# Batch 0's values through a casting DMA, key sums from a column of ones, and one copy moved to VectorE, in a fused attention and swish-MLP kernel

## The chip, the cores and the metric

The kernel runs on one core of one Trainium2 chip. The time is the device time of one execution in microseconds; the figure given for a kernel is the median of several runs. TensorE (PE) multiplies matrices, its weight loads are listed as PEld; VectorE (DVE), ScalarE (ACT) and GpSimd (POOL) work on tiles in SBUF and PSUM; SyncE (SP) issues most of the DMAs.

## What is computed

Linear attention over 8 batches, 8 heads, 576 positions and head size 64, whose result goes through an MLP with a swish that has a slope of its own for each of 2048 hidden columns:

```python
q_s = exp(q - max(q, -1)); q_s = q_s / sum(q_s, -1)      # softmax over the 64 channels
k_s = exp(k - max(k,  2)); k_s = k_s / sum(k_s,  2)      # softmax over the 576 positions
kv  = einsum('bhsd,bhse->bhde', k_s, v)
x   = einsum('bhsd,bhde->bhse', q_s, kv)                 # -> 4608 tokens x 512
h   = x @ w_in                                           # 512 -> 2048
out = (h * sigmoid(beta * h)) @ w_out                    # 2048 -> 512
```

All inputs and the output are float32 in DRAM; the kernel multiplies in bf16 and leaves the two maxima out, which cancel.

## The kernel before, in words

**Tiles.** A batch's 8 heads are handled as 4 pairs (`hp` 0 to 3). K and V of a pair lie as 128 partitions x 9 blocks (`NG`) x 64. `KF`, `VF`, `QF` hold the float32 inputs of a batch (two buffers each, chosen by the batch's parity), `EK` and `EQ` the bf16 exponentials, `VB` the bf16 values. A row of `VB` is `VW` = 66 wide: 64 values and two more that GpSimd sets to one (L230), so that one matmul with 65 columns gives K^T V and, in column 64, the sum of the keys. `kvd` (L391) scales the product by the reciprocal of that sum into `KVD`; `out_mm` (L426) multiplies it with the transposed queries `QT` into a 128 x 512 piece of `XT`, one for each pair. `pass1_mm` (L627) multiplies the four pieces of `XT` with `WIN` into the 16 tiles of h (`f` 0 to 15), ScalarE makes the swish of each (L637), `pass2_group` (L706) multiplies with `WOUT`. The nine slabs `t` are the eight batches' first 512 positions, and slab 8 the positions that are left over.

**Order.** Nothing is scheduled by the machine: each engine runs its instructions in the order in which the program adds them, and `Program` (L46) works out which semaphores an instruction waits for from the keys that it reads and writes. The attention of a later batch is woven into the matmuls of an earlier slab: `todo` holds pairs of a slot number and a step, and `tick` (L740) runs the steps that are due after each matmul.

**Batch 0, the head of the kernel.** There is no earlier slab to hide it in. SP issues Q in 4 chunks (L283), K in 4 (L529), beta (L532) and V in 4 (L534). `exp_q` and `exp_kh` run on ScalarE (L594 to L600), `norm_main` (L322) divides the queries by their sums: a reduction and a reciprocal on VectorE, a multiplication on VectorE or, for pairs 1 and 3, on GpSimd (L602, L608). `t_steps` (L364) transposes a pair on TensorE and copies it to `QT`. Key sums are taken apart from the products here: `ksum` (L500) multiplies by column 64 of `VB` alone, `ksum_inv` (L506) takes reciprocals. V is turned to bf16 by `cast_v` (L343): pairs 0 and 1 on VectorE, 2 and 3 on ScalarE (L621 to L623). `kv_mm` (L511) makes the products. `warm` (L493) issues matmuls whose result nobody reads.

**The weights.** `load_win` (L556) brings w_in in five pieces through DMAs issued on GpSimd that turn float32 into bf16; the first waits for the last chunk of batch 0's K. Piece 0 has columns 0 to 255 (`f` 0 and 1), piece 1 the next 256, pieces 2 to 4 have 512 each (`f` 4 to 7, 8 to 11, 12 to 15). `load_wout` (L539) on SP brings w_out as float32; its first DMA waits for piece 2 of w_in (`wgate`, L561), and behind it on SP are the loads of batch 1 (L764 to L768) and of the later batches. `scale_wout` (L546) multiplies w_out on VectorE by the reciprocal of beta.

**Slab 1.** `attn_late(2)` (L483) prepares batch 2 beside slab 1's second matmuls. Its four copies of PSUM to `XT` run on VectorE for pairs 0 to 2 and on ScalarE for pair 3 (L487). In front of the latter in ScalarE's order stand the exponentials of batch 3 (L801 to L809).

Of the kernel before, what the change touches and what calls it, by code (L numbers as in the profile page):

```python
# [158 lines left out]
def bass_efficient_attn_shen__then__act_swish_beta_kernel(  # L159
# [12 lines left out]
    with ExitStack() as es:  # L172
        def sb(name, shape, dt):
            return es.enter_context(nc.sbuf_tensor(name, shape, dt))
# [33 lines left out]
        IDB = sb("IDB", [128, 128], BF16)  # L208
        WARM = sb("WARM", [128, 512], BF16)
        DUMMY = sb("DUMMY", [128, 8], F32)  # L210

        PS = [es.enter_context(nc.psum_tensor(f"PS{i}", [128, 512], F32)) for i in range(8)]
        HB = (0, 1, 2)
# [5 lines left out]


        add(DVE, lambda e: e.memset(WARM[:, :], 0.0), w=["warm"])  # L221
        add(POOL, lambda e: e.iota(IOTA[:, :], [[1, 128]], base=0, channel_multiplier=-1,
                                   allow_small_or_imprecise_dtypes=True), w=["iota"])
        add(POOL, lambda e: e.tensor_scalar(IDB[:, :], IOTA[:, :], 0.0, None, ALU.is_equal),
# [1 line left out]
        add(POOL, lambda e: e.tensor_scalar(IDF[:, :], IOTA[0:4, 0:4], 0.0, None, ALU.is_equal),  # L226
            r=["iota"], w=["idf"])

        def homes(i):
            add(POOL, lambda e: e.memset(VB[i][:, :, :, D:VW], 1.0), w=[("vone", i)])  # L230
            for e_ in range(2):
                z = EK[i][64 * e_:64 * e_ + 64, :, :, 64 * (1 - e_):64 * (2 - e_)]
                add(POOL, lambda e, z=z: e.memset(z.bitcast(F32), 0.0), w=[("ekz", i, e_)])
            for e_ in range(2):
                z = KVD[i][64 * e_:64 * e_ + 64, :, 64 * (1 - e_):64 * (2 - e_)]
                add(POOL, lambda e, z=z: e.memset(z.bitcast(F32), 0.0), w=[("kvz", i, e_)])
# [35 lines left out]
        def load_v(b, split=1, cs=None):  # L272
            load_pairs("vf", vt_h, VF, b, split, cs)
# [80 lines left out]
        def bank(pool=MB):  # L354
            rot[0] += 1
            return pool[rot[0] % len(pool)]
# [126 lines left out]
        def attn_late(b):  # L483
            s = spread(kv_steps(b, (0, 1)), 99, 103) + spread(kv_steps(b, (2, 3)), 105, 109)
            x = []
            for hp in range(NHP):
                x += out_step(b, hp, MB, ACTE if hp == 3 else DVE)  # L487
            return s + spread(x, 110, 123)

        def spread(steps, lo, hi):  # L490
# [8 lines left out]

        def ksum(b, hp, kb):  # L500
            for j in range(NG):
                l, r_, ke, kv, ko = kv_rows(b, hp, j)
                mm(PS[kb][:, hp:hp + 1], l, r_[:, D:D + 1], j == 0, j == NG - 1, r=ke + ko,
                   w=[("ps", kb)], bk=kb)

        def ksum_inv(b, kb, hp0, n):  # L506
# [3 lines left out]

        def kv_mm(b, hp, bk, n):  # L511
            for j in range(NG):
                l, r_, ke, kv, ko = kv_rows(b, hp, j)
                mm(PS[bk][:, VW * n:VW * n + D], l, r_[:, 0:D], j == 0, j == NG - 1,
                   r=ke + kv, w=[("ps", bk)], bk=bk)

        def out_now(b, hp, bk, eng):
# [12 lines left out]
        for i, n in enumerate((2, 4)):  # L530
            a = bass.AP(beta_h, FG[n][0], [[128 * n, len(FG[n])], [1, 128 * n]])
            add(SP, lambda e, i=i, a=a: e.dma_start(BT[i][:, :], a), w=[("bt", i)],  # L532
                slot=f"bt{i}")
        load_v(0, 4)  # L534
        STAGE = (WST[0], WST[1], O2S[1], O2S[0])
        SKEY = ([("wst", 0)], [("wst", 1)], [("o2", 1, u) for u in range(4)],
                [("o2", 0, u) for u in range(4)])
# [18 lines left out]
        def load_win(c):  # L556
            c0, n = WCH[c]
            a = bass.AP(win_h, c0, [[DFF, 128], [128 * DFF, NM], [1, n]])
            add(POOL, lambda e, c0=c0, n=n, a=a: e.dma_start(WIN[:, :, c0:c0 + n], a),  # L559
                w=[("win", c)], slot=f"win{c}", after=P.writer[("kf", 0, 3)] if c == 0 else ())  # L560
            if c == 2:  # L561
                wgate.append(P.ops[-1])

# [26 lines left out]

        homes(0)
        kb = bank(HEAD)
        warm(8, 0)
        exp_q(0)  # L594
        exp_kh(0, 0, 1, 0)
# [7 lines left out]
        go(t_steps(0, (0,), HEAD))  # L603
        warm(3, 0)
        norm_main(0, 2, 1)
        load_win(0)
        load_win(1)
        norm_main(0, 3, 1, POOL)  # L608
        for c in range(2, len(WCH)):
            load_win(c)  # L610
        homes(1)
        go(t_steps(0, (1,), HEAD))
        warm(2, 0)
        go(t_steps(0, (2,), HEAD))
# [3 lines left out]
        ksum(0, 1, kb)  # L618
        ksum_inv(0, kb, 0, 2)
        warm(3, 0)  # L620
        cast_v(0, 0, DVE, 2)  # L621
        cast_v(0, 2, ACTE)
        cast_v(0, 3, ACTE)  # L623

        orot = [0]

# [36 lines left out]
        kv_mm(0, 0, 3, 0)  # L663
        kv_mm(0, 1, 3, 1)
        kvd(0, 0, 3, 0, 2)
        go(t_steps(0, (3,), (1,)))
        ksum(0, 2, kb)
        ksum(0, 3, kb)
        ksum_inv(0, kb, 2, 2)
# [54 lines left out]
        for t in range(NSLAB):  # L724
            todo = []
            if t == 0:
                todo = [(TT[k_], lambda k_=k_: go(t_steps(1, (2 * k_, 2 * k_ + 1), (1 + k_,))))
                        for k_ in range(2)]
                todo += [(113, lambda: o2_evac(0, 0, 3, ACTE)), (114, lambda: o2_evac(0, 1, 4, ACTE))]
                todo.append((106, lambda: (norm_main(1, 2, 1), norm_main(1, 3, 1))))  # L730
                todo += spread(kv_steps(1, (0, 1), (0,)), 115, 117) + spread(kv_steps(1, (2, 3), (1,)), 122, 125)
                todo += [(121, lambda: out_now(1, 0, 7, DVE)), (126, lambda: out_now(1, 1, 3, ACTE))]
            elif t == 1:
                todo = spread(outr_steps(1), 97, 101) + attn_late(2)
            elif t < 7:
                todo = attn(t + 1)
            todo = sorted(todo, key=lambda x: -x[0])
            slot = [0]

            def tick():  # L740
                slot[0] += 1
                while todo and todo[-1][0] <= slot[0]:
                    todo.pop()[1]()

            if 2 <= t < 7:
                for hp in (0, 2):
                    norm_main(t + 1, hp, 2)
                    t_dma(t + 1, hp, 2)
                if t % 2 == 0:
                    norm_rem(t // 2)  # L750
                    tr_dma(t // 2)
                if t == 2:
                    load(5)
            elif t == 1:
                for hp in range(NHP):
                    cast_v(2, hp)
            if t < 2:
                slot[0] = NM * FIRST[t]
            for f in range(FIRST[t] if t < 2 else 0, NF):
                pass1_tile(t, f, tick)  # L760
            if t == 0:
                for c in range(4):
                    scale_wout(c)
                for cs in ((0, 1), (2, 3)):  # L764
                    load_main("qf", qt_h, QF, 1, 4, cs)
                    load_k(1, 4, cs)
                load_v(1, 4)
                load_qrem(0)  # L768
                load(2)
                for hp in (0, 2):  # L770
                    exp_q(1, hp, 2)
                    exp_kh(1, hp, 2, 0)
                    exp_kh(1, hp, 2, 1)
                for hp in range(2):
                    norm_main(1, hp, 1, POOL if hp == 1 else DVE)
                for hp in range(NHP):
                    cast_v(1, hp)
                pass2_group(0, (0, 1, 2, 3), (3, 4, 5, 6), tick)
                while todo:
                    todo.pop()[1]()  # L780
                at = first_tiles(1, FIRST[1])
                add(ACTE, lambda e: e.activation(DUMMY[:, 2:3], WARM[:, 0:1], ACT.Silu),
                    r=["warm"], w=["dummy"])
                at(0)
                out_now(1, 2, 7, DVE)
                at(1)
                out_now(1, 3, 3, ACTE)
                at(2)
                at(3)
                o2_evac(0, 2, 5, DVE)  # L790
                o2_evac(0, 3, 6, DVE)
                store(0)
                load(3)
                continue
            nb = [t + 2] if t + 2 < B else []
            if t == 1:
                nb = [2, 3]
                exp_qr(0)
                norm_rem(0)
                tr_dma(0)  # L800
            for b in nb:  # L801
                exp_q(b)
                if b == 2:
                    for hp in range(2):
                        norm_main(2, hp, 1, POOL)
                    t_dma(2, 0, 2)
                if b % 2 == 1:
                    exp_qr(b // 2)
                exp_k(b, step=2)  # L809
                if b > 3:  # L810
                    for hp in range(NHP):
                        cast_v(b, hp)
                if b + 2 < B and t > 1:
                    load(b + 2)
            for u in range(4):
                pass2_group(t, (u,), (OB[orot[0] % 2],), tick)
                orot[0] += 1
                if t == 1 and u == 0:
                    for hp in range(2, 4):
                        norm_main(2, hp, 1, POOL)  # L820
                    t_dma(2, 2, 2)
                    for hp in range(NHP):
                        cast_v(3, hp)
                    load(4)
            while todo:
                todo.pop()[1]()
            if t < 8:
                store(t)
# [30 lines left out]
```

## Time and profile before

| | |
|---|---|
| median of 5 runs | 290.9 us (290.62 to 292.34) |
| profiled execution | 291.54 us, of which its span is 289.8 us |
| PE busy | 280.7 us, 97% of the span, 1595 matmuls |
| ACT, DVE, POOL busy | 178.6, 110.4, 39.1 us |
| moved by DMA | 47.97 MB, 166 GB/s over the span |

Busy time is the union of an engine's instructions. A matmul's end is modelled, so that consecutive ones overlap in the record: 62 with 512 columns lie within 14.02 us, about 0.226 us apart, though each is listed with 0.38 us. A short idle time of TensorE can therefore hide under the listed duration. For each instruction that began after idle time the timeline names in brackets that time and what ended it. The chain of work that ended last is followed back from the last instruction, at each step to what released it. DMA rates count the bytes written; a DMA that turns float32 into bf16 reads twice as many.

### The profile page before, as it was taken

Reading aid. Unit: us, or ns where it says so; the run is one execution under the profiler, and the core shown is the slowest. Engines: PE = TensorE matmul, PEld = TensorE weight load, DVE = VectorE, ACT = ScalarE, POOL = GpSimd, SP = SyncE. Lnnn points to the kernel's source line nnn. Section 1 sums busy time; section 2 is a strip of 40 time slices with the busy share of each in tenths; the row PEclk is TensorE's granted clock in tenths of the full one; section 3 lists DMA queues with packets and bytes.
Section 4 is the critical chain, followed back from the end, with each engine's and each line's share of the span. In section 5 each row is a group of like instructions: output and inputs, shape, how many; then the busy total and the mean of one; then the engine's idle time right before and its main releaser. Section 6 shows DMA issues by size and latency. Waiting matters only on the chain.

```text
span 289.8 us, 3873 instructions
## 1 busy us (share of the span) xinstructions
PE 280.7 (97%) x1595; PEld 137.6 (47%) x1595; DVE 110.4 (38%) x197; ACT 178.6 (62%) x240; POOL 39.1 (13%) x57
## 2 busy tenths in 40 slices
PE   6999989999999999999999999999999999999994
PEld 2545445454545444544454445544554455445441
DVE  4640667206783156305560555054804300110011
ACT  5858665889997973689268916892670086017500
POOL 5740014123603021400050000000000000000000
PEclk9999999999999999999999999999999999999999
DMA  7999999995699999705990015000810030012022
GB/s 223 297 192 345 404 357 308 347 385 138 172 391 218 341 330 402 125 0 150 368 226 0 2 71 147 2 0 36 166 36 1 0 147 0 0 55 92 0 72 72
DMA packets 41292, 47.97 MB, mean 166 GB/s; under 512 B 20149, under 2 KB 30903, under 8 KB 39866
## 3 DMA queue, kind: packets, MB, share of 16 engines
q1 hardware_dynamic: 38314, 45.10, 50.5%
q0 software_dynamic: 2640, 2.10, 5.0%
q10 hardware_dynamic: 320, 0.52, 0.5%
q8 instruction: 12, 0.20, 0.3%
q14 instruction: 6, 0.05, 0.0%
HBM read 36.71 MB, written 9.44 MB: 159 GB/s over the span
## 4 chain that ended last, share of the span: by engine, by line
PE 83%; DMA 8%; SPq 6%; POOL 1%; issue 1%; DVE 0%; ACT 0%
PE PS L362 82%; SPq L249 4%; DMA VF<-in_v_dram 3%; DMA WIN<-in_moe_w_in_dram 3%; DMA KF<-in_k_dram 2%; SPq L259 1%; SPq L543 1%; POOL WIN L559 0%; POOL EQ L331 0%; DVE O2S L690 0%; POOL VB L348 0%; ACT XT L437 0%; PE PS L360 0%
## 5 line engine op out<-in xcount | busy, mean ns | idle before, releaser
L637 ACT ACTIVATE GT<-PS,BETA 128x512 bf16<-128x512 f32 x144 | 98.1, 688 | 79.7 <-PE PS L362 79.5
L362 PE MATMUL PS<-XT,WIN 128*128 128x512 bf16 x576 | 132.8, 380 | 0.8 <-ACT XT L437 0.7
L362 PE MATMUL PS<-WOUT,GT 128*128 128x512 bf16 x576 | 133.3, 379 | 0.0
L362 PEld LDWEIGHTS PS<-XT,WIN 128*128 128x128 bf16 x576 | 62.2, 110 | 60.1 <-DVE XT L520 1.5
L362 PEld LDWEIGHTS PS<-WOUT,GT 128*128 128x128 bf16 x576 | 54.5, 98 | 62.2 <-DVE O2S L690 0.2
L690 DVE COPY O2S<-PS 128x512 f32<-128x512 f32 x34 | 23.2, 686 | 111.3 <-PE PS L362 111.3
L362 PE MATMUL PS<-VB,EK 128*128 128x65 bf16 (+2 forms) x324 | 38.0, 196 | 0.7 <-DVE VB L348 0.4
L348 POOL CAST VB<-VF 128x576 bf16<-128x576 f32 x28 | 21.0, 751 | 73.0 <-DMA VF<-in_v_dram 42.2
L362 PEld LDWEIGHTS PS<-VB,EK 128*128 128x128 bf16 x324 | 24.2, 103 | 9.5 <-DVE VB L348 1.3
L304 ACT ACTIVATE EK<-KF 64x1152 bf16<-64x1152 f32 x24 | 27.8, 1157 | 0.4
L292 ACT ACTIVATE EQ<-QF 128x512 bf16<-128x512 f32 x32 | 18.0, 619 | 5.6 <-DMA QF<-in_q_dram 5.4
L329 DVE TENSOR_REDUCE QS<-EQ 128x8 f32<-128x512 bf16 (+1 forms) x22 | 20.2, 918 | 3.4 <-ACT EQ L292 3.2
L437 DVE CAST XT<-PS 128x512 bf16<-128x512 f32 x23 | 15.8, 691 | 10.9 <-PE PS L362 10.9
L331 DVE TENSOR_TENSOR EQ<-EQ,QI 128x1024 bf16<-128x1024 bf16 (+1 forms) x15 | 15.8, 1052 | 0.5
L362 PE MATMUL PS<-QT,KVD 128*128 128x512 bf16 x32 | 12.3, 395 | 0.2 <-DVE KVD L399 0.2
L331 POOL TENSOR_TENSOR EQ<-EQ,QI 128x512 bf16<-128x512 bf16 x7 | 7.3, 1045 | 35.6 <-DVE QI L330 35.4
L314 ACT ACTIVATE EK<-KF 64x1152 bf16<-64x1152 f32 (+1 forms) x10 | 9.5, 964 | 1.5 <-DMA KF<-in_k_dram 1.4
L362 PE MATMUL PS<-WARM 128*128 128x512 bf16 x17 | 8.2, 628 | 1.2 <-DVE WARM L221 1.2
L399 DVE TENSOR_TENSOR KVD<-PS,RC 64x128 bf16<-64x128 f32 (+1 forms) x22 | 7.7, 350 | 3.3 <-PE PS L362 2.7
L337 DVE TENSOR_REDUCE QRS<-EQR 128x8 f32<-128x512 bf16 x4 | 2.7, 679 | 14.4 <-ACT EQR L319 14.4
L548 DVE TENSOR_SCALAR WOUT<-WST,RB 128x512 bf16<-128x512 f32 x8 | 3.3, 480 | 10.2 <-DMA WST<-in_moe_w_out_dram 10.2
L292 ACT ACT_TABLE_LOAD x5 | 6.4, 1283 | 0.1
(47 smaller groups left out, 77.6 us busy)
## 6 DMA issues: line engine op xcount, KB each, us to landing
out_dram<-O2S SPq DMA_DIRECT2D x8, 1024.0 KB, 5.4
KF<-in_k_dram SPq DMA_DIRECT2D x6, 1152.0 KB, 9.2
VF<-in_v_dram SPq DMA_DIRECT2D x6, 1152.0 KB, 11.4
QF<-in_q_dram SPq DMA_DIRECT2D x6, 1024.0 KB, 7.4
KF<-in_k_dram SPq DMA_DIRECT2D x8, 288.0 KB, 6.8
VF<-in_v_dram SPq DMA_DIRECT2D x8, 288.0 KB, 7.5
QF<-in_q_dram SPq DMA_DIRECT2D x8, 256.0 KB, 8.1
WST<-in_moe_w_out_dram SPq DMA_DIRECT2D x2, 1024.0 KB, 8.7
```

What stands on the lines that cost most here:

```text
L249: add(SP, lambda e, c=c: e.dma_start(dst(bufs[i], c * n, n), src(th, b, c * n, n)), w=[(name, i, hp) for hp in range(c * n // 2, (c + 1) * ...
L292: add(ACTE, lambda e, o=o, a=a: e.activation(o, a, ACT.Exp), r=[("qf", i, hp)], w=[("eq", i, hp)])
L304: add(ACTE, lambda e, o=o, a=a: e.activation(o, a, ACT.Exp), r=[("kf", i, h) for h in hps], w=[("ek", i, h, e_) for h in hps])
L314: add(ACTE, lambda e: e.activation(o, a, ACT.Exp), r=[("kf", i, h) for h in hps], w=[("ek", i, h, e_) for h in hps])
L329: add(DVE, lambda e: e.tensor_reduce(s_, a, AX.X, ALU.add), r=ks, w=[("qs", i, hp0)])
L331: add(eng, lambda e: e.tensor_tensor(a, a, vb, ALU.mult), r=ks + [("qi", i, hp0)], w=ks)
L348: add(eng, lambda e: (e.copy if eng == ACTE else e.tensor_copy)(o, a), r=[("vf", i, h) for h in hps] + [("vone", i)], w=[("vb", i, h) for ...
L362: add(PE, lambda e: e.matmul(o, l, r_, start=start, stop=stop), r=r, w=w, bank=[bk])
L399: add(DVE, lambda e, o=o, a=a, s_=s_: e.tensor_tensor(o, a, s_, ALU.mult), r=[("ps", bk)] + [("rc", i, h) for h in hps], w=[("kvd", i, h, ...
L437: add(eng, lambda e: (e.copy if eng == ACTE else e.tensor_copy)(XT[i][:, hp, :], PS[bk][:, :]), r=[("ps", bk)], w=[("xt", i, hp)], bank=[bk])
L637: add(ACTE, lambda e: e.activation(GT[:, f, :], PS[bk][:, :], ACT.Silu, scale=BETA[:, f:f + 1]), r=[("ps", bk), "beta"], w=[("gt", f)], ba ...
L690: add(eng, lambda e: (e.copy if eng == ACTE else e.tensor_copy)(O2S[t % 2][:, u, :], PS[bk][:, :]), r=[("ps", bk)], w=[("o2", t % 2, u)], ...
```

## The change

Batch 0's V no longer comes by SP as float32 into `VF` to be cast by VectorE and ScalarE. Two DMAs issued on GpSimd, of two pairs each, write it as bf16 straight into `VB[0]`, without the two extra columns: 576 values of a pair in a row, at the start of the buffer. The first waits for the third chunk of Q. `kv_mm` reads this layout through an access pattern of its own. `ksum` multiplies by a new tile `ONE`. The columns of ones of `VB[0]` are set in slab 1, before batch 2's casts (`v_ones(0)`), those of `VB[1]` where they were, by a call of their own.

With it: the multiplication of pair 3's queries moves from GpSimd to VectorE; w_in's first piece no longer waits for K; its five issues stand behind the second of V's; pair 3's transposes move ahead of the products and two `warm` matmuls are added behind them; the copy of batch 2's pair 3 moves from ScalarE to VectorE.

```diff
+        ONE = sb("ONE", [128, 2], BF16)
...
+        add(DVE, lambda e: e.memset(ONE[:, :], 1.0), w=["one"])
...
+        def v_ones(i):
+            add(POOL, lambda e: e.memset(VB[i][:, :, :, D:VW], 1.0),
+                w=[("vone", i)] + [("vb", i, hp) for hp in range(NHP)])
+
         def homes(i):
-            add(POOL, lambda e: e.memset(VB[i][:, :, :, D:VW], 1.0), w=[("vone", i)])
...
-                x += out_step(b, hp, MB, ACTE if hp == 3 else DVE)
+                x += out_step(b, hp, MB)
...
-                l, r_, ke, kv, ko = kv_rows(b, hp, j)
-                mm(PS[kb][:, hp:hp + 1], l, r_[:, D:D + 1], j == 0, j == NG - 1, r=ke + ko,
+                l, _, ke, _, _ = kv_rows(b, hp, j)
+                mm(PS[kb][:, hp:hp + 1], l, ONE[:, 0:1], j == 0, j == NG - 1, r=ke + ["one"],
...
-                mm(PS[bk][:, VW * n:VW * n + D], l, r_[:, 0:D], j == 0, j == NG - 1,
+                r_ = bass.AP(VB[0], hp * KW + j * D, [[NHP * NG * VW, 128], [1, D]])
+                mm(PS[bk][:, VW * n:VW * n + D], l, r_, j == 0, j == NG - 1,
...
-        load_v(0, 4)
...
-                w=[("win", c)], slot=f"win{c}", after=P.writer[("kf", 0, 3)] if c == 0 else ())
+                w=[("win", c)], slot=f"win{c}")
...
+        def load_vb(hp):
+            a = bass.AP(vt_h, hp * 2 * HS, [[KW, 128], [2 * HS, 2], [1, KW]])
+            o = bass.AP(VB[0], hp * KW, [[NHP * NG * VW, 128], [KW, 2], [1, KW]])
+            add(POOL, lambda e: e.dma_start(o, a), w=[("vb", 0, hp), ("vb", 0, hp + 1)],
+                slot=f"vb{hp}", after=P.writer[("qf", 0, 2)])
+
+        load_vb(0)
         warm(8, 0)
...
         norm_main(0, 2, 1)
-        load_win(0)
-        load_win(1)
-        norm_main(0, 3, 1, POOL)
-        for c in range(2, len(WCH)):
+        norm_main(0, 3, 1)
+        load_vb(2)
+        for c in range(len(WCH)):
             load_win(c)
         homes(1)
+        v_ones(1)
...
         warm(3, 0)
-        cast_v(0, 0, DVE, 2)
-        cast_v(0, 2, ACTE)
-        cast_v(0, 3, ACTE)
+        go(t_steps(0, (3,), (1,)))
+        warm(2, 0)
...
         kvd(0, 0, 3, 0, 2)
-        go(t_steps(0, (3,), (1,)))
         ksum(0, 2, kb)
...
             elif t == 1:
+                v_ones(0)
                 for hp in range(NHP):
                     cast_v(2, hp)
```

## The prediction, made before the result was known

> **What bounds the kernel now.** I read the shares of busy time first: TensorE is busy for 97% of the span, so only what opens or closes a hole in its stream can move the end. Next I read the chain that ended last, in order of time (start, length, what):
>
> ```profile
> 4.25 5.45 DMA KF<-in_k_dram
> ...
> 12.74 8.89 DMA WIN<-in_moe_w_in_dram
> ...
> 29.14 4.55 SPq L249
> ...
> 35.26 9.75 DMA VF<-in_v_dram
> ...
> 45.06 0.68 POOL VB L348
> ...
> 47.34 34.10 PE PS L362 x210
> ...
> 81.45 0.59 ACT XT L437
> ...
> 82.09 203.81 PE PS L362 x1117
> ```
>
> Up to 45.7 us the chain is not TensorE at all. It is a line of transfers: K, w_in's third piece (landing at 12.74 + 8.89 = 21.63, which lets w_out start), then the loads of batch 1 up to V, whose cast lets TensorE go on. SP's issue of 4.55 us shows a full queue in front of it. After that the chain is TensorE with one foreign link, ScalarE's copy at 81.45. The stretches (TensorE's busy time ahead, DMA share and GB/s last) confirm that transfers are the limit there:
>
> ```profile
> 6.00:11.00 5.00, 4.76 (x24) 2.71 (x25) 4.17 (x11) 4.23 (x7) 2.04 (x3) 1.00 1.03 393
> 11.00:16.00 5.00, 4.61 (x72) 3.26 (x71) 2.69 (x7) 2.70 (x4) 4.93 (x7) 1.00 1.20 182
> 16.00:23.00 7.00, 6.66 (x35) 2.80 (x33) 2.37 (x7) 5.09 (x8) 1.98 (x4) 1.00 1.23 200
> 28.00:42.00 14.00, 13.38 (x65) 6.38 (x63) 8.98 (x21) 8.84 (x12) 0.91 (x1) 1.00 1.03 393
> ```
>
> The DMA engines are never free from 6 us on; 200 GB/s written by the casting loads of w_in is 400 read, the rate of the plain loads. Last, TensorE's timeline at the three places that count:
>
> ```profile
> 11.66 1.44 PE L362 MATMUL PS<-WARM 128*128 128x512 bf16 x3
> 13.50 1.14 PE L362 MATMUL PS<-VB,EK 128*128 128x64 bf16 x18 [0.40 <-DVE VB L348]
> 14.45 0.61 PE L360 MATMUL PS<-IDB,EQ 128*128 128x128 bf16 x4
> ...
> 17.22 0.64 PE L362 MATMUL PS<-XT,WIN 128*128 128x512 bf16 x2
> ...
> 42.18 0.40 PE L360 MATMUL PS<-IDB,EQ 128*128 128x128 bf16 x4 [0.80 <-POOL EQ L331]
> ...
> 45.79 0.20 PE L362 MATMUL PS<-VB,EK 128*128 128x65 bf16 x1 [0.34 <-POOL VB L348]
> ...
> 80.62 0.81 PE L362 MATMUL PS<-XT,WIN 128*128 128x512 bf16 x3
> 82.09 1.25 PE L362 MATMUL PS<-XT,WIN 128*128 128x512 bf16 x5 [0.66 <-ACT XT L437]
> ```
>
> The holes at 42.18 and 45.79 both end when batch 1's inputs have come. A head that ends earlier only makes them longer; one up to 0.80 us later is absorbed in the first.
>
> **Part 1, the copy at 81.45: -0.81 us.** TensorE issues a 512-column matmul every 0.226 us (62 in 14.02). Three from 80.62 on are out by 81.28; the fourth waits for pair 3's copy until 82.09: 0.81 lost. ScalarE makes that copy late because batch 3's exponentials (76.73 to 81.43) are ahead of it. Its product is made by 79.06, and VectorE's rows around it are
>
> ```profile
> 77.92 1.28 DVE L437 CAST XT<-PS 128x512 bf16<-128x512 f32 x2
> 80.82 0.69 DVE L690 COPY O2S<-PS 128x512 f32<-128x512 f32 x1 [1.63 <-PE PS L362]
> ```
>
> so a copy of 0.69 fits from 79.20 to 79.89 into an idle time of 1.63. Without that cover it would delay the output copy, which has the next store behind it and no matmul. What is late next is ScalarE's table load: it starts when the exponentials end, 0.6 earlier than now, and the first h tile then frees its bank at about 83.34, just when TensorE comes to reuse it. So 0.6 to 0.81 is gained; I take 0.8. Nothing after 82.09 has a hole that could take it back.
>
> **Part 2, the head of TensorE: 0.** Removed are one cast on VectorE (1.38), two on ScalarE (1.25, which has 2.74 us idle behind them) and the wait of 0.60 between the last `warm` matmul (due at about 12.90) and 13.50. Added are two `warm` matmuls; pair 3's transposes only change places with the products. The eight first `warm` matmuls take 3.60 us, 0.43 apart, and those at 11.66 too: at this rate two cost 0.85, and the head ends 0.25 later, under the 0.80 at 42.18. Here a rule speaks: the Trainium skill (TensorE: Matmul & The Clock Gate, The HAM clock gate) says that TensorE runs at half rate until a window of some 3.4 us was busy throughout. The granted clock reads 1.00 in every stretch, but the spacing halves at 17.2 to 17.5, some 3.7 us after the hole before 13.50. If closing that hole brings the full rate one window sooner, about 13.9, the head ends some 1.2 us earlier (by the rule) instead of 0.25 later (by the row). Either way the sum gets nothing: w_in's third piece lands at 21.63, the last at 14.48 + 14.1 = 28.6, and by 0.226 a matmul TensorE wants them at about 21.7 and 28.9. Only 0.3 us of an earlier head passes these, and 42.18 takes that.
>
> The small edits are covered: pair 3's multiplication costs VectorE 0.69 (GpSimd: 1.06) in an idle time of 1.51 before 11.97; the memset of `ONE` falls before 4.37, where VectorE waits 3.22; `v_ones(0)` is 0.2 us on GpSimd in 8.98 idle; four issues less on SP (1.82 us) save nothing, as SP waits 14.4 us for w_in afterwards. `ONE` leaves the 36 key-sum matmuls as they are.
>
> **Part 3, the order of the transfers: -0.6 us, between -1.1 and +0.5.** V's 1.18 MB are read either way. By the queues' totals the plain queue spends 0.505 x 289.8 us on 45.1 MB, 3.24 us for one MB; the casting queue 0.050 x 289.8 on 4.2 MB read, 3.45. As a cast V costs 0.25 us more, 0.5 if its rows share the engines badly with K. Against that stands the start of the casting queue. Written GB/s from 8 to 24 us in slices of 0.4:
>
> ```profile
> GB/s 409 382 387 380 421 392 426 403 346 216 92 138 147 138 161 168 178 147 157 175 184 189 174 202 197 207 200 200 236 195 197 197 207 205 207 205 205 197 202 294
> ```
>
> From 12.0 to 17.2 it stays below 200; the shortfalls sum to 552 GB/s-slices, 552 / 200 x 0.4 = 1.1 us. In the new order this queue begins at about 7 us with V's first half (issued once Q's third chunk is in at 5.6; a first byte 1.7 us after issue, as at 10.00), while K still fills the engines. All of it hidden is -1.1; I take half, as part of it belongs to w_in's short first rows. The whole line behind it (21.63, w_out, batch 1 at 42.18 and 45.79) then moves by that, and TensorE has the 0.80 to follow.
>
> The new wait for Q holds up what is queued behind it on GpSimd: pair 1's multiplication (due at 7.01, the issue ends at about 6.6), V's second half and w_in's five issues. K is slowed by sharing, its last chunk from 9.70 to 11 or 11.5; its exponentials then end at about 13.8 instead of 12.47, and the key sums of pairs 2 and 3 want them at 14 to 15.
>
> **Sum.** The span 289.8 becomes 289.8 - 0.8 - 0.6 = 288.4, the profiled execution 291.54 - 1.4 = 290.1. That execution is 0.64 above the median of the runs; the median goes from 290.9 to 289.5.
>
> **Rivals.** *All of the start is hidden* and the head is early enough to follow: -0.8 - 1.1 - 0.3, 288.7. For it: K and V overlap fully; against it: the slow rows of w_in remain. *The line stays where it is*, because the slowest of the 16 DMA engines sets every landing (V of batch 1 takes 9.75 us in a full queue) and has the same bytes: -0.8 + 0.2, 290.3, no change. The copy's 0.8 is then all of it, and the cast V does nothing for the time. *Slower: GpSimd's issues are starved.* The Trainium skill (SBUF — State Buffer, A bandwidth-pool intuition that's wrong) says that a DMA issued by GpSimd took 3.1 us beside a VectorE copy instead of 0.62. Two more issues now stand in front of w_in, at 5.6 and 8.1 us, where VectorE works without pause. By the rule two struck issues cost 5 us, of which 2 is lead (V lands at 12.9, w_in could have been issued at 10): 3 us late, 290.9 - 0.8 + 3 = 293.1. By the row nothing: GpSimd's three issues at 12.74 took 2.50 us together, the one beside VectorE's cast at most 0.25 more than the rest. The rival decides once w_in is over 0.8 us late; I side with the row.
>
> **How the numbers follow.** My forecast has 0.36 (289.0 to 290.0), the full gain 0.27, the unmoved line 0.22, starvation 0.15. A change of 0.5%, 1.45 us (about what a measurement of this kernel can tell from none), is 289.45: half of the first case and all of the second are below it (0.45). Of starvation 0.11 ends over 292.35. That leaves 0.44 for the same. The range 288.4 to 291.1 takes in the first three cases and leaves out most of the fourth.
>
> **What would show it.** The ScalarE link at 81.45 gone from the chain and no hole at 80 to 82; w_in's third piece in by about 21.0; the hole at 42.18 no shorter than 0.6; the head's first XT matmul between 16.0 and 17.5. It is wrong if that third piece lands after 22.4, if K's exponentials hold up the key sums, or if a new hole opens before 28 us that 42.18 cannot absorb.

## The result, and the profile after

| | before | changed |
|---|---|---|
| median | 291.05 us (80 runs, 289.72 to 294.37) | 290.41 us (43 runs, 289.13 to 291.93) |
| ratio to before | | 0.9970, 95% interval 0.9957 to 0.9983: 0.87 us less, 0.49 to 1.25 |
| profiled execution, its span | 291.54, 289.8 | 290.28, 288.5 |

Faster, but by less than the 0.5% that I had named. The ratio leaves out slow runs, those over 1.5% above the kernel's fastest, and is what I go by below; the two medians lie 0.64 us apart. The line numbers of the changed kernel are a few higher: L362 is L367, L331 is L336, L437 is L442. TensorE's timeline at the places that the prediction spoke of:

```profile
8.79 0.61 PE L365 MATMUL PS<-IDB,EQ 128*128 128x128 bf16 x4 [0.93 <-POOL EQ L336]
...
10.04 0.63 PE L365 MATMUL PS<-IDB,EQ 128*128 128x128 bf16 x4
...
13.58 0.63 PE L365 MATMUL PS<-IDB,EQ 128*128 128x128 bf16 x4
14.00 1.06 PE L367 MATMUL PS<-WARM 128*128 128x512 bf16 x2
14.86 1.17 PE L367 MATMUL PS<-VB,EK 128*128 128x64 bf16 x18
...
17.88 0.59 PE L367 MATMUL PS<-XT,WIN 128*128 128x512 bf16 x2 [0.29 <-ACT XT L526]
...
41.28 0.61 PE L365 MATMUL PS<-IDB,EQ 128*128 128x128 bf16 x8
...
46.30 0.40 PE L365 MATMUL PS<-IDB,EQ 128*128 128x128 bf16 x4 [0.38 <-DVE EQ L336]
...
80.04 1.89 PE L367 MATMUL PS<-XT,WIN 128*128 128x512 bf16 x8
```

The holes at 42.18 and 45.79 are gone, and so is the one behind 80.62: eight matmuls now follow each other from 80.04. Two holes are new. One, at 8.8, makes the head later and not earlier (first XT matmul 17.88 for 17.22). The other, of 0.38 at 46.3, ends with VectorE's multiplication of batch 1's pair 3. The chain that ended last tells the same:

```profile
1.76 4.60 DMA QF<-in_q_dram
...
7.69 1.05 POOL EQ L336
...
43.48 1.20 DVE EQ L336
...
45.55 0.70 DVE EQ L336
...
46.69 237.90 PE PS L367 x1327
```

No transfer stands in it after Q. Up to 46 us TensorE is bound by its own head and then by VectorE's chain of normalisations; from there to the last matmul it is TensorE alone.

### The profile page after: what moved, and what is told of

Read it like the earlier page. It is cut to its first block, busy times and chain, and to the rows that moved or that the text cites. A ratio compares the mean times of both kernels' runs of the same rounds, so it can differ in the third digit from the quotient of the medians.

```text
span 288.5 us, 3872 instructions
## 1 busy us (share of the span) xinstructions
PE 280.4 (97%) x1597; PEld 137.7 (48%) x1597; DVE 111.4 (39%) x199; ACT 176.7 (61%) x237; POOL 38.5 (13%) x58
## 4 chain that ended last, share of the span: by engine, by line
PE 94%; DVE 2%; DMA 2%; issue 1%; POOL 0%; SPq 0%; ACT 0%
PE PS L367 92%; DMA QF<-in_q_dram 2%; PE PS L365 1%; DVE EQ L336 1%; DVE QS L334 0%; POOL EQ L336 0%; SPq L254 0%; DVE XT L526 0%; DVE QT L385 0%; DVE O2S L701 0%; ACT XT L526 0%; DVE QI L335 0%; POOL VB L602 0%
## 5 line engine op out<-in xcount | busy, mean ns | idle before, releaser
L367 PE MATMUL PS<-WOUT,GT 128*128 128x512 bf16 x576 | 133.3, 379 | 0.0
L367 PE MATMUL PS<-XT,WIN 128*128 128x512 bf16 x576 | 132.7, 380 | 0.4 <-ACT XT L526 0.3
L367 PEld LDWEIGHTS PS<-XT,WIN 128*128 128x128 bf16 x576 | 62.2, 109 | 59.6 <-DVE XT L526 1.5
L367 PEld LDWEIGHTS PS<-WOUT,GT 128*128 128x128 bf16 x576 | 54.5, 98 | 62.1 <-DVE O2S L701 0.2
L367 PE MATMUL PS<-VB,EK 128*128 128x65 bf16 (+1 forms) x288 | 36.3, 197 | 0.0
L353 POOL CAST VB<-VF 128x576 bf16<-128x576 f32 x28 | 20.3, 725 | 73.2 <-PE PS L367 45.8
L367 PEld LDWEIGHTS PS<-VB,EK 128*128 128x128 bf16 x288 | 22.7, 102 | 7.8 <-issue 0.9
L442 DVE CAST XT<-PS 128x512 bf16<-128x512 f32 x24 | 16.4, 690 | 10.9 <-PE PS L367 10.9
L336 DVE TENSOR_TENSOR EQ<-EQ,QI 128x1024 bf16<-128x1024 bf16 (+1 forms) x16 | 17.5, 1092 | 0.6
L367 PE MATMUL PS<-QT,KVD 128*128 128x512 bf16 x32 | 11.8, 380 | 0.0
L336 POOL TENSOR_TENSOR EQ<-EQ,QI 128x512 bf16<-128x512 bf16 x6 | 6.2, 1041 | 34.6 <-DVE QI L335 34.3
L367 PE MATMUL PS<-WARM 128*128 128x512 bf16 x19 | 9.3, 629 | 1.2 <-DVE ONE L223 1.2
L526 ACT CAST XT<-PS 128x512 bf16<-128x512 f32 x4 | 2.2, 588 | 8.3 <-PE PS L367 8.2
```

Source lines behind the costliest of these rows:

```text
L336: add(eng, lambda e: e.tensor_tensor(a, a, vb, ALU.mult), r=ks + [("qi", i, hp0)], w=ks)
L353: add(eng, lambda e: (e.copy if eng == ACTE else e.tensor_copy)(o, a), r=[("vf", i, h) for h in hps] + [("vone", i)], w=[("vb", i, h) for ...
L367: add(PE, lambda e: e.matmul(o, l, r_, start=start, stop=stop), r=r, w=w, bank=[bk])
L442: add(eng, lambda e: (e.copy if eng == ACTE else e.tensor_copy)(XT[i][:, hp, :], PS[bk][:, :]), r=[("ps", bk)], w=[("xt", i, hp)], bank=[bk])
```

## Where the difference sits in time

The start of slab 1's first XT matmul cuts the span in two. It is this row, of the kernel before and of the changed one:

```profile
50.11 0.81 PE L362 MATMUL PS<-XT,WIN 128*128 128x512 bf16 x3
...
49.54 0.81 PE L367 MATMUL PS<-XT,WIN 128*128 128x512 bf16 x3
```

Where I say that a hole is so long "by the starts", I mean the time between two matmuls' starts beyond the usual spacing; it does not depend on the modelled ends. The part behind slab 1's start does not vary from profile to profile of kernels with the same copy (one exception, win_waits, where TensorE waited 0.48 us by the starts at 71.0); the part ahead of it does. From the traces of all profiles, in us:

| kernel | w_in's third piece lands | w_out complete | V of batch 1, pair 1 | slab 1 starts | from there to the end |
|---|---|---|---|---|---|
| before | 21.63 | 36.85 | 45.01 | 50.11 | 239.64 |
| before_again | 21.89 | 37.20 | 46.66 | 51.92 | 239.64 |
| copy_only | 20.61 | 35.22 | 42.66 | 48.41 | 238.92 |
| changed | 20.27 | 35.55 | 43.42 | 49.54 | 238.92 |
| after_again | 20.02 | 35.36 | 43.09 | 49.20 | 238.92 |
| rest_only | 19.82 | 35.08 | 43.73 | 48.84 | 239.65 |
| norm_early | 20.28 | 35.52 | 43.47 | 49.00 | 238.93 |
| order_only | 18.63 | 34.47 | 43.24 | 48.34 | 239.64 |
| order_copy | 18.73 | 34.01 | 42.23 | 49.31 | 238.91 |
| order_copy_norm | 19.05 | 34.28 | 41.70 | 49.09 | 238.91 |
| win_waits | 20.56 | 35.79 | 43.29 | 48.98 | 239.30 |
| mul_first_norm | 20.13 | 35.40 | 44.41 | 49.57 | 238.92 |
| no_warm_norm | 21.19 | 36.54 | 44.66 | 50.03 | 238.93 |
| order_t3 | 19.02 | 33.66 | 41.51 | 47.29 | 238.92 |

copy_only is the kernel before up to slab 1, and its slab 1 starts 1.7 us earlier than in the one profile of before and 3.5 earlier than in the other. Each row is one execution, and not always a typical one: the profiled run of before_again is 2.5 us above the median of its runs, that of copy_only 1.1 below. A single pair of profiles therefore proves nothing about this part.

## The experiments

Four kernels ran on each of three chips, each beside the kernel before on the same chip; ratios are to that.

**copy_only**: before, with the copy alone.

```diff
-                x += out_step(b, hp, MB, ACTE if hp == 3 else DVE)
+                x += out_step(b, hp, MB)
```

> The kernel before with one edit: batch 2's fourth copy on VectorE. Theory A (the copy is worth its 0.8 us and the new order of the transfers adds some 0.4 on average): 0.8 us below the kernel before, so 0.1 to 0.5 above the changed kernel. Theory B (all of the gain is the copy): as fast as the changed kernel, 0.9 below before. Both: the hole at 82 us is gone from TensorE's stream and those at 42 and 46 us stay as they were, together about 1.1 us.

Measured: 290.19 us, ratio 0.9970 (0.9939 to 1.0001), the changed kernel's ratio to the last digit. The times cannot tell the theories apart; the table can for the copy: 239.64 against 238.92, 0.72 us. The four profiles with the copy on ScalarE have 239.64 or 239.65, nine of the ten with it on VectorE 238.91 to 238.93. That the holes at 42 and 46 us stay was wrong: in this profile two of 0.16 and 0.17 by the starts are left (at 43.8 and 45.2), with the same code as before. Inputs and head had been early by chance.

**rest_only**: changed, with the copy on ScalarE.

```diff
-                x += out_step(b, hp, MB)
+                x += out_step(b, hp, MB, ACTE if hp == 3 else DVE)
```

> The changed kernel with batch 2's fourth copy back on ScalarE: the order of the transfers, V's casting DMAs and the head alone. Theory A: 0.1 to 0.6 us below the kernel before; the last of w_in's third piece lands about a microsecond before 21.6, and the hole of 0.8 at 42 us is gone. Theory B: no difference to before within 0.2 us; the landing of the third piece lies anywhere between 20 and 22 us. A third, C (the head is later for the wait of GpSimd on Q, and eats the transfers' gain): the third piece lands early, but TensorE's first XT matmul is 0.5 us later than 17.2, and the time is that of before.

Measured: 290.71 us, ratio 0.9975 (0.9945 to 1.0004): 0.73 us less, between 1.6 less and 0.1 more, which excludes neither theory. Its TensorE timeline is the cleanest test of part 2:

```profile
9.52 0.39 PE L365 MATMUL PS<-IDB,EQ 128*128 128x128 bf16 x4
...
15.61 0.61 PE L367 MATMUL PS<-XT,WIN 128*128 128x512 bf16 x2 [0.63 <-ACT XT L526]
...
27.44 3.64 PE L367 MATMUL PS<-XT,WIN 128*128 128x512 bf16 x16 [0.39 <-DMA WIN<-in_moe_w_in_dram]
...
40.41 0.40 PE L365 MATMUL PS<-IDB,EQ 128*128 128x128 bf16 x4 [0.47 <-POOL EQ L336]
...
43.67 0.20 PE L367 MATMUL PS<-VB,EK 128*128 128x65 bf16 x1 [0.49 <-POOL VB L353]
```

In this execution TensorE ran at the full rate from about 9.4 us on (the four transposes took 0.39 us; the same four at 10.04 in the changed kernel 0.63), and the first XT matmul came at 15.61; the same head takes 17.88, 17.70 and 17.49 in the changed kernel, after_again and norm_early. Of 2.3 us of lead over the changed kernel 0.7 is left at slab 1. The rest went into waits for w_in's last piece, for batch 1's queries and for its V. Theory C, a head that is too late, cannot be judged by an execution whose full rate came so early.

**order_only**: before, with w_in's issues early and together; V stays float32 on SP with its casts.

```diff
-                w=[("win", c)], slot=f"win{c}", after=P.writer[("kf", 0, 3)] if c == 0 else ())
+                w=[("win", c)], slot=f"win{c}")
...
-        load_win(0)
-        load_win(1)
-        norm_main(0, 3, 1, POOL)
-        for c in range(2, len(WCH)):
+        norm_main(0, 3, 1)
+        for c in range(len(WCH)):
```

> The kernel before with w_in's five issues earlier: the first no longer waits for the last chunk of K, pair 3's multiplication is on VectorE so that nothing stands between the five; V stays float32 on SP, with its casts. If an early start of the casting queue is what moves the line of transfers (my prediction's step), w_in's third piece lands 0.5 to 1 us earlier than 21.6 and the time falls by 0.3 to 0.6. If it is the cast V, that is fewer bytes written and one queue after the other, that does it, nothing moves, or V lands later because w_in shares the engines with it and the head is some 0.5 us late, hidden under the hole at 42 us.

Measured: 290.17 us, ratio 0.9953 (0.9926 to 0.9979), 1.4 us less, without the copy. The third piece landed at 18.63, three microseconds before the 21.63 of the kernel before and 1.6 before the changed kernel. GpSimd's timeline in the changed kernel

```profile
6.67 0.95 POOL L602 DMA_DIRECT2D VB<-in_v_dram  x1 [1.92 <-DMA QF<-in_q_dram]
7.69 1.04 POOL L336 TENSOR_TENSOR EQ<-EQ,QI 128x512 bf16<-128x512 bf16 x1
8.68 0.76 POOL L602 DMA_DIRECT2D VB<-in_v_dram  x1
9.44 3.73 POOL L564 DMA_DIRECT2D WIN<-in_moe_w_in_dram  x5
```

and in order_only

```profile
6.88 1.04 POOL L331 TENSOR_TENSOR EQ<-EQ,QI 128x512 bf16<-128x512 bf16 x1 [1.92 <-DVE QI L330]
7.86 3.96 POOL L559 DMA_DIRECT2D WIN<-in_moe_w_in_dram  x5
```

looks alike, but the transfers do not. Written GB/s from 8 to 24 us in slices of 0.4 us, of the changed kernel

```profile
GB/s 403 400 322 238 160 181 130 150 164 158 157 184 178 163 120 92 125 173 179 184 195 205 204 209 205 210 200 238 197 195 202 205 210 197 210 207 207 207 236 305
```

and of order_only

```profile
GB/s 317 346 363 376 412 391 403 369 415 379 312 231 207 200 197 196 200 201 210 209 210 210 202 207 205 246 192 192 205 202 202 205 207 207 210 292 351 371 389 376
```

Plain transfers show about 400 here and casting ones 200 at the same reading rate. In the changed kernel the plain queue is out of work at about 9.6 us, and the casting queue then needs until 16 to come to 200. In order_only the plain queue works until about 13, since V is still in it. The first casting packets come at 11.9, among the last plain ones, and the total goes from the plain level to the casting one without a dip. The queues' megabytes from 8 to 18 us show what this is worth (q0 casts, q1 is the plain queue; the changed kernel first, then order_only):

```profile
q0 software_dynamic: 1951, 1.47, 102.3%
q1 hardware_dynamic: 248, 0.48, 12.3%
...
q0 software_dynamic: 1678, 1.15, 76.2%
q1 hardware_dynamic: 815, 1.64, 44.4%
```

A casting queue reads twice what it writes, so 3.4 MB were read in the changed kernel and 3.9 in order_only, where 400 GB/s would be 4.0. This holds in all profiles: 3.1 to 3.6 in the three with the old order, 3.3 to 3.5 in the seven with the cast V, 3.9 to 4.0 in the four with order_only's edit. The prediction had put a part of the loss down to w_in's short first rows; order_only has the same rows and hardly a loss. Why the casting queue is slow at first stays open. In every profile it held 190 GB/s only after GpSimd's last issue had ended (0.3 to 4.1 us after), so the issuing itself may set the pace; no run separates the two.

**norm_early**: changed, with the normalisation of batch 1's pairs 2 and 3 at slot 103.

```diff
-                todo.append((106, lambda: (norm_main(1, 2, 1), norm_main(1, 3, 1))))
+                todo.append((103, lambda: (norm_main(1, 2, 1), norm_main(1, 3, 1))))
```

> The changed kernel with the queries of batch 1's pairs 2 and 3 normalised three slots earlier in slab 0 (slot 103 for 106), in VectorE's order ahead of the copy that waits for TensorE. The changed kernel has a new hole of 0.38 us (0.54 by the starts) at 46.3, which ends with pair 3's multiplication on VectorE. If VectorE's order is the cause, this multiplication ends 0.9 us sooner, the hole is gone and the time is 0.4 to 0.5 below the changed kernel. If the landing of batch 1's inputs is still the limit there, another hole, at V's cast, takes its place and the time stays within 0.2.

Measured: 289.85 us, ratio 0.9938 (0.9908 to 0.9968), 0.9 us below the changed kernel's ratio with intervals that just overlap. That is not yet a gain: after_again, the changed kernel itself, has 0.9931 on another chip. The trace must show it. The hole at 46.3 is gone (eight transposes in a row), and what the second outcome named is in its place with about 0.4 us by the starts (43.82 and 44.62):

```profile
44.08 0.74 PE L367 MATMUL PS<-VB,EK 128*128 128x65 bf16 x9
...
45.56 0.61 PE L365 MATMUL PS<-IDB,EQ 128*128 128x128 bf16 x8
```

Slab 1 starts 0.54 earlier than in the changed kernel, but 0.39 of that is the head (first XT matmul 17.49 for 17.88); the exchange of one hole for another gives the rest. VectorE's rows say why the normalisation had been late. In the changed kernel (first listing, with one row of GpSimd) VectorE stood still for 2.29 us at a copy that waited for TensorE, with the reduction behind it; in norm_early (second) the reduction goes first, and starts when ScalarE's exponentials are there. The order is not the only cause: the multiplication at 43.48 took 1.20 instead of 0.69 beside GpSimd's cast of V, and this half microsecond alone is about the hole of 0.54.

```profile
41.93 0.69 DVE L385 COPY QT<-PS 128x1024 bf16<-128x1024 bf16 x1 [2.29 <-PE PS L365]
42.53 0.68 DVE L334 TENSOR_REDUCE QS<-EQ 128x8 f32<-128x512 bf16 x1
43.24 0.20 DVE L335 RECIPROCAL QI<-QS 128x8 f32<-128x8 f32 x1
43.47 0.67 POOL L353 CAST VB<-VF 128x576 bf16<-128x576 f32 x1 [0.21 <-DMA VF<-in_v_dram]
43.48 1.20 DVE L336 TENSOR_TENSOR EQ<-EQ,QI 128x512 bf16<-128x512 bf16 x1
```

```profile
41.59 0.69 DVE L334 TENSOR_REDUCE QS<-EQ 128x8 f32<-128x512 bf16 x1 [1.98 <-ACT EQ L297]
```

**before_again**, the kernel before without an edit.

> The kernel before, unchanged, for a second profile and as a measure of the scatter. In the profiles so far the time from slab 1's first matmul to the end is fixed by the code alone (239.64 us with the copy on ScalarE, 238.92 with it on VectorE), while the start of slab 1 lies between 48.3 and 50.1 us, even for copy_only, whose code is that of before up to there (48.4 against 50.1). If chance sets the line of transfers, this profile again has 239.6 behind slab 1's start, and the start lies anywhere in that range.

Measured: 290.83 us, ratio 0.9980 (0.9946 to 1.0015): a kernel against itself, 0.6 us apart at twelve runs. Slab 1 started at 51.92, beyond the range that I had given.

**after_again**, the changed kernel without an edit.

> The changed kernel, unchanged, for a second profile. If the cast V moves the line of transfers for good, w_in's third piece lands near 20.2 us as in the two other profiles with it (20.3, 19.8 and 20.3 with norm_early) against 21.6 and 20.6 without. If only chance does, it may be as late as 21.6. In either case 238.9 us lie between slab 1's start and the end.

Measured: 289.81 us, ratio 0.9931 (0.9902 to 0.9959). The third piece landed at 20.02, and 238.92 us lie behind slab 1's start, as expected.

**order_copy**: order_only's edit and copy_only's together.

> order_only with the copy on VectorE as well: the two gains without the cast V. order_only measured 0.9 us below before (its interval 0.6 to 2.1), and w_in's third piece landed at 18.6. If the early issues of w_in move the line and the copy's 0.72 adds to it, this is 1.0 to 1.6 below before, faster than the changed kernel, and the cast V was not needed. If order_only's gain was chance, it is as fast as copy_only, 0.7 to 0.9 below before.

Measured: 290.07 us, ratio 0.9940 (0.9913 to 0.9966), 1.75 us less. The third piece at 18.73. On the same chip it equals after_again within the intervals: the cast V is not needed for such a time, but I could not show order_copy to be faster. Slab 1 started no earlier (49.31 for 49.20) although V of batch 1 had come 0.9 earlier: TensorE was held at 46.1 at the same transposes as in the changed kernel (0.35 us by the starts).

**order_copy_norm**: order_copy with norm_early's edit.

> order_copy with the queries of batch 1's pairs 2 and 3 normalised at slot 103. In order_only's profile no hole ends with that multiplication (only 0.21 at V's cast, at 44.0), so 0 to 0.3 us below order_copy; if TensorE arrives earlier than in that profile, up to 0.5. It is my candidate for the fastest of all.

Measured: 289.72 us, ratio 0.9910 (0.9868 to 0.9953). From 21 us to slab 1 the starts of its matmuls show no hole but three of 0.21 us, in each of which one record is missing from that trace: the head alone sets the end.

**win_waits**: changed, with w_in waiting for K again.

```diff
-                w=[("win", c)], slot=f"win{c}")
+                w=[("win", c)], slot=f"win{c}", after=P.writer[("kf", 0, 3)] if c == 0 else ())
```

> The changed kernel with w_in's first piece waiting for the last chunk of batch 0's K again, as before. In the changed kernel the five issues start at 9.4, after V's second half, and K is complete at 9.8 to 10.0, so the wait costs half a microsecond of issue in a queue that still has V in front. If the line of transfers moved because w_in is issued early and without the multiplication between its pieces, the third piece stays near 20.2 us and the time within 0.3 of the changed kernel. If leaving out the wait for K was what moved it, the piece is back at 21 to 21.6 and the holes at 42 and 46 us open again.

Measured: 290.32 us, ratio 0.9967 (0.9931 to 1.0002); third piece at 20.56, w_out complete at 35.79. Against the changed kernel's 0.9970 this shows no worth in dropping the wait, with V ahead of w_in in the queue. A hole of 0.4 at 20.6 and one of 1.1 at 41.1 did open, but mainly because full rate came early here (first XT matmul 15.86 for 17.88); the third piece was only 0.3 later than in the changed kernel.

**mul_first_norm**: norm_early, with V's first half behind the multiplication.

```diff
-        load_vb(0)
         warm(8, 0)
...
         norm_main(0, 1, 1, POOL)
+        load_vb(0)
```

> norm_early with V's first half issued behind the multiplication of pair 1 on GpSimd, not ahead of it. In the changed kernel that multiplication began at 7.69 (6.98 was due) since GpSimd sat waiting for Q, and TensorE had a hole of 0.93 us at 8.8. If this is what made the head 0.3 us later than before, the hole is gone, the first XT matmul comes 0.6 earlier (about 17.1), and of that at most 0.4 is seen in the time, the holes that norm_early has left. V's first half is issued 1.3 us later: if V becomes the limit, there is a hole at the first products, at 14.

Measured: 290.42 us, ratio 0.9971 (0.9947 to 0.9996), no gain over norm_early; the second outcome, at another place than I had named. The multiplication began at 6.74 and the transposes behind it at 7.84, 0.95 earlier than in the changed kernel; the hole ahead of them stayed (0.91), as TensorE ran at the full rate from 5.9 us and came early too. The products of V's first half began at 12.19, those of the second at 14.93, after a hole of 1.63 us for V. Behind that hole TensorE was back at the slow spacing until about 18.6, and two holes of 0.77 and 0.59 by the starts at 44.2 and 45.2 followed.

**no_warm_norm**: norm_early without the two added matmuls.

```diff
         go(t_steps(0, (3,), (1,)))
-        warm(2, 0)
```

> norm_early without the two warm matmuls that the change adds behind pair 3's transposes. At the slow spacing they cost 0.85 us of the head. If the head counts, XT's first matmul is up to 0.85 earlier and the time up to 0.4 lower (holes of 0.4 are left in norm_early). If the two keep TensorE busy for the full rate, the spacing halves later than at 16.3 to 16.6, and the head is no earlier, or later.

Measured: 290.18 us, ratio 0.9950 (0.9921 to 0.9979). Inconclusive: full rate came at about 10.8 in this profile, so the two matmuls would have cost half, and w_in's third piece was late (21.19). In norm_early, by the spacing of its 64-column products, the full rate had begun at about 14.9, ahead of the 16.3 that I had read.

**order_t3**: order_copy_norm, with pair 3's transposes ahead of the products.

```diff
         cast_v(0, 3, ACTE)
+        go(t_steps(0, (3,), (1,)))
...
         kvd(0, 0, 3, 0, 2)
-        go(t_steps(0, (3,), (1,)))
```

> order_copy_norm with pair 3's transposes ahead of the first products, as the change has them; V still float32 by SP with its casts. order_copy_norm has no hole left after 20 us, so TensorE is bound by its head, which has a hole of 0.9 to 1.5 us before the products at 13.75, where V's cast on VectorE ends. The transposes (0.43) go into that hole: the first XT matmul 0.4 earlier, and the time 0.3 to 0.45 below order_copy_norm, the fastest of all. If the line of transfers is the limit once more, the gain turns into a hole at 44.

Measured: 288.91 us, ratio 0.9914 (0.9878 to 0.9949), the lowest median of all, 2.5 us below the kernel before and with no casting DMA for V. Against order_copy_norm, on another chip, the ratio shows no difference. The profiled run is 0.9 below the kernel's own median, and its head ran at the full rate for longer than order_copy_norm's, so the transposes' part in it stays open. Its TensorE timeline has the last listed hole over 0.2 us at 12.66:

```profile
11.93 0.39 PE L360 MATMUL PS<-IDB,EQ 128*128 128x128 bf16 x4
12.66 2.10 PE L362 MATMUL PS<-VB,EK 128*128 128x64 bf16 x45 [0.34 <-DVE VB L348]
...
15.96 0.59 PE L362 MATMUL PS<-XT,WIN 128*128 128x512 bf16 x2
16.72 0.61 PE L362 MATMUL PS<-QT,KVD 128*128 128x512 bf16 x2 [0.17 <-DVE KVD L399]
```

w_out was complete at 33.66, V of batch 1 in at 41.51, and slab 1 began at 47.3.

## Why the prediction was right, and which term was off

**The copy, -0.8: right.** It is 0.72 in all profiles but win_waits. Matmul for matmul the hole closed by 0.83 (I had counted 0.81 with the mean spacing of 0.226, which takes in short waits; the usual one is 0.216). Of this 0.1 came back in slab 2, most of it where TensorE waited for the first h tile to free its bank. That is the next-late term that I had named: ScalarE's table load came 0.63 earlier, counted from slab 1's start.

**The head, 0: right, with one cost missed.** A lead of the head was worth little: of 2.3 us 0.7 were left at slab 1 in rest_only. The row gave 0.25 later, the rule 1.2 earlier; the trace shows 0.3 to 0.7 later, and not for the `warm` matmuls alone. I had GpSimd's new wait end at 5.6, ahead of the multiplication at 7.01. Q's third chunk came at 6.37, the issue ended at 7.6, the multiplication began at 7.69, and TensorE waited 0.93 for it. The full rate then came at about 16.5 instead of 17.3, not at the 13.9 of the rule, and gave part of it back. The Trainium skill's rule on the clock gate (TensorE: Matmul & The Clock Gate, The HAM clock gate) says that the window runs freely, not from the kernel's start. The profiles agree in that the moment scatters (the same head had full rate at 9.4 in rest_only and at about 16.5 in the changed kernel); no run shows the window itself.

**The order of the transfers, -0.6: the direction right, the reason wrong, the size too large.** Five of the seven profiles with the cast V have the third piece between 19.8 and 20.3 us (win_waits 20.56, no_warm_norm 21.19); the three without it and in the old order have it at 20.6, 21.6 and 21.9. So the line did come earlier, by about a microsecond in the mean, though copy_only's w_out was as early as those with the cast V. But the step that said why, that the casting queue begins at 7 us under K and hides its slow start, failed. It began at 9 as K ran out, K was hardly slowed (last chunk 9.98 for 9.70), and the slow start was all there: from 9.6 to 16.4 us the shortfalls from 200 sum to 707 GB/s-slices, 1.4 us, more than the 1.1 before. The gain came from the other end. Each of these DMAs is reported 16 times, once by each DMA engine, and what waits goes on with the last report (w_out's issue at 21.65). For the third piece the reports came from 18.04 to 21.63 before, and from 18.52 to 20.27 after: the first is later, the last earlier, and the mean no earlier (18.82 before, 19.16 after, 17.89 in order_only). Why they are more even with V in the casting queue stays open. order_only, order_copy, order_copy_norm and order_t3 show what hiding the start is really worth: third piece at 18.6 to 19.1, w_out complete at 33.7 to 34.5 instead of 35.2 to 37.2. In all four there was plain traffic in front of the casting queue until GpSimd had issued all of w_in, and V was that traffic. The cast V took it away.

**"TensorE has the 0.80 to follow": the step that cut the gain.** In the pair of profiles the line came 1.3 us earlier at w_out and 1.6 at V, while slab 1 started 0.57 earlier. The head was 0.3 later, and I had not asked what is late next at 42.18: VectorE's normalisation of pairs 2 and 3, held in its order behind a copy that waits for TensorE and stretched by GpSimd's cast. The sum closes: by the starts the two holes of the kernel before were 0.96 and 0.50; of these 1.46 us 0.29 went to the later head and 0.54 into the new hole, which leaves 0.63 for the 0.57 measured. norm_early moves this hole to V's cast, and order_copy_norm, whose inputs come 1.7 us earlier there, has neither. My sign "the hole at 42.18 no shorter than 0.6" did not come, and it contradicted the sum: a line that comes 0.6 earlier can be a gain only by shortening that hole. The sign for the head, a first XT matmul by 17.5, was missed as well, with 17.88.

In the profiles the sum was near: -1.4 foretold, 290.28 - 291.54 = -1.26 found. That is luck in part: the profiled execution of before had been 0.49 above the median of its 80 runs, that of the changed kernel 0.13 below its own. By the ratio all that is not the copy is 0.87 - 0.72 = 0.15, with the interval -0.2 to 0.5, so a gain from the line is not shown in the times. The median of 290.41 lies above my own forecast of 289.0 to 290.0 and within the wider range, which took in an unmoved line too.

Of the rivals, starved issues on GpSimd did not show: the issue at 8.68, beside VectorE's work, took 0.76 us like the others, and w_in's third piece came at 20.27, not late. "The line stays and the copy is all of it" foretold 290.3 and is, on the medians, the nearest, though the line did not stay.

## What to carry to other kernels

Where two streams meet, an input that comes a microsecond earlier is worth only what the next-latest wait leaves: look for the second-last arrival at the waiting instruction, and at what stands in front of it in its engine's order, before you book a stall as gained. Moving a load from one DMA queue to another moves bytes and can also take away what was hiding the other queue's start. And find the marker behind which the time does not scatter: one pair of profiles, cut there, gave the copy to some 0.02 us (one of fourteen profiles was off, by 0.38), which twelve runs of whole times could not.

## What the runs showed of the hardware that was not expected

- VectorE instructions were stretched when GpSimd worked beside them. The same 128x512 multiplication took 0.69 us alone, 1.27 at 8.01 beside GpSimd's multiplication (7.69 to 8.73) and 1.20 at 43.48 beside its cast (43.47 to 44.14); both ended 0.54 or 0.55 after GpSimd's instruction. The cast of two pairs of V took 1.38 us before, beside a multiplication of GpSimd, and 0.82 in order_t3, where it began ahead of GpSimd's next two memsets; these took 2.66 us instead of the 2.16 of before. The Trainium skill (SBUF — State Buffer, SBUF: two separate sides) names a pair of ports that the two engines share and that only one of them holds at a time; these rows agree.
- With early issues the casting queue did not share with the plain one: in order_only w_in was issued from 7.86 on, and its first packets moved at 11.9, when V was nearly through and GpSimd's last issue had just ended (11.8). In the changed kernel V's first casting packets moved 2.0 us after the issue at 6.67. Which of the two held w_in back is open.
- TensorE's full rate began for good anywhere between 9.4 us (rest_only) and about 19 (order_copy_norm) in profiles of nearly the same head. It can also come and go: in six profiles the four transposes at about 6.0 ran 0.056 us apart, at the full rate, and the slow 0.107 was back at 8.2 in copy_only; order_t3 had 512-column matmuls 0.427 apart again at 15.0. rest_only and the changed kernel, whose code is the same up to slab 1, differ by 2.3 us at the first XT matmul for it.
